# Attention stage: the log of the softmax sum goes into the row that carries the maximum; four q/k sets; one exponential for the last query tile

## The chip, the cores and the metric

One core of a Trainium2 chip runs the whole program in one launch. The metric is device microseconds of one execution. PE is TensorE, DVE is VectorE, ACT is ScalarE, POOL is GpSimd, and SP is the queue from which nearly all DMAs are issued.

## The reference, cut to what matters

Attention over 4 batches of 8 heads, 576 tokens, head size 64, float32, followed by two feed-forward parts (a dense one in `w_in`, `w_out`, then a routed one with 8 experts):

```python
cum    = np.cumsum(np.log(np.clip(f, 1e-4, 1.0)), axis=-1)
scores = q @ k.T / 8 + cum[..., :, None] - cum[..., None, :]
scores = np.where(causal, -1e9, scores)
scores = scores - np.max(scores, axis=-1, keepdims=True)
attn   = np.exp(scores)
attn   = attn / (np.sum(attn, axis=-1, keepdims=True) + 1e-9)
x      = attn @ v
x      = leaky_relu(x @ w_in) @ w_out          # 2304 tokens, 512 -> 2048 -> 512
out    = routed experts(x)                     # not touched by the change
```

## The kernel before, in words

The change lies in the first stage, attention, which also turns the first half of `w_in` (64-bit floats in memory) into 32-bit parts beside its own work. The heads go in 16 pairs, `n` = 0 to 15. The two heads of a pair lie in partitions 0 to 63 and 64 to 127. A pair has three steps:

- `prepare`: loads q and k (tile `x`), turns them on PE, and splits the result into a rounded part and a rest (`qh`, `ql`, `kh`, `kl`); ACT makes the rounded part, DVE the rest. These and two tiles of extra rows (`qr`, `kr`) make a set; there are three sets, and pair `n` uses set `(n + 2) % 3`. The rows of the cumulated logs reach `kr` by a DMA from `cumd`.
- `offsets`: scores with the queries in the partitions, in four parts (query tiles 1 and 2; 3 and 0; tile 4 in two halves of 288 keys). DVE adds the mask and takes minus the row's maximum (`kept`, `nm`; it shows as CUSTOM_DVE), ACT takes the exponential and sums it (`sm`). `rows` splits `nm` into two parts (`xh`), turns them on PE, copies them (`xr`) and writes them by two DMAs into rows of `qr`. `inverse` adds the two sums of tile 4, adds 1e-9 and takes the reciprocal (three DVE instructions on `sm`). A turn on PE, an ACT copy (`xi`), one DMA to memory (`invd`) and two that read it back over 64 partitions each fill `R`.
- `attend`: scores with the keys in the partitions, where the product with `kr`, `qr` adds the cumulated logs and minus the maximum. ACT takes the exponential (`P`), POOL clears what lies above the diagonal, PE multiplies by v (`vt`) into `av`, for 320 and then 256 queries. `finish` multiplies `av` by `R` on DVE, POOL rounds the product and subtracts (two instructions, tile `xt`), and a DMA stores both to `xd`.

All tiles of PSUM in this stage come from one ring of four (`s`). `weight_ops` loads one 128x256 piece of `w_in` (tile `w`, ring `w64`), runs three DVE instructions (`wbits`) and three on POOL (`wsq`, `wst`); there are 16 pieces here. `x_ops` loads the input of the next stage (`X` from `xd`) in two DMAs of 1 MB.

The order on each engine is written by a planner (`Plan.order`): every operation has an engine, an assumed duration, what it needs, the buffers it takes, and a rank. The planner walks through assumed time, and on each engine that is free it takes the ready operation of the lowest rank. `MOVE` holds the time it assumes from a DMA's issue to its end. `NEAR` lets PE prefer matmuls of one kind. Ranks count 12 for each pair: `prepare` of pair `n` has `12n + ZP`, `offsets` `12n + ZO`, `attend` `12n + ZA`. On the chip each engine then runs its instructions strictly in that order. Nearly all of them are issued by one helper and so stand under line 66 in the profile: they are told apart by tile.

The next stage starts with `x @ w_in` on PE (`h<-X,wh`) while `w_out` pieces are loaded (`w<-in_moe_w_out`).

Of the kernel before, what the change touches and what calls it, by code (L numbers as in the profile page):

```python
# [12 lines left out]
FT = mybir.dt.float32  # L13
# [17 lines left out]
WB = 40  # L31
W64 = 2, 6, 4
# [14 lines left out]
NEAR = 7.5  # L47
NEARB = 5
ZN = 2.5, 0, 0, 0
ZM = 0, 0, 0, 0  # L50
NK = 4
SB = 4
# [33 lines left out]
class Plan:  # L86
# [5 lines left out]
    MOVE = 650, 950  # L92
# [128 lines left out]
def tile_kernel(ctx, tc, q, k, v, f, w_in, w_out, w_gate, w1, w2, out):  # L221
# [12 lines left out]
    invd = drp.tile([B * H // 2, 12, 128], FT, name="invd")  # L234
# [25 lines left out]
    def weight_ops(op, pieces, z, st, low_on, keep=None):  # L260
# [7 lines left out]
        def chunk(c, src):  # L268
            m = {}

            def load():
                m["w"] = raw[0].tile([128, 256, 2], I32, name="w64", tag="w64", bufs=raw[1])
                sp.dma_start(m["w"].rearrange("p a b -> p (a b)"), src)
# [22 lines left out]
            o = op("sp", 450, load, (), z, ["w64"], (), 728)  # L296
# [59 lines left out]
    def w_in_ops(op, half, c, z, low_on):  # L356
        st = {}
        weight_ops(op, [(256 * u, w_in[128 * c:128 * c + 128, 2048 * half + 512 * u:2048 * half + 512 * u + 512]) for u in range(4)], z, st, low_on)
        return st
# [153 lines left out]
    with ExitStack() as c1:  # L513
# [4 lines left out]
        raw[:] = at, W64[0]  # L518
# [23 lines left out]
        def load_f():  # L542
            pre["ft"] = at.tile([hd, S], FT, name="ft", tag="xt", bufs=2)
            pre["cn"] = [at.tile([hd, S], FR, name="cn", tag="R", bufs=2) for _ in range(2)]
            sp.dma_start(pre["ft"], f.rearrange("b h s -> (b h) s"))
# [13 lines left out]
        o = op("sp", 450, load_f, (), -1000, ["R", "R", "xt"], (), 30)  # L559
        xb, fb = o.got[:2], o.got[2]  # L560
# [5 lines left out]
        for l in range(2):  # L566
            o = op("vec", 500, lambda l=l: negate(l), [o], -1000, (), [cb, xb[l]])
            cums.append(op("sp", 450, lambda l=l: sp.dma_start(cumd[l], pre["cn"][l].bitcast(FT)), [o], -1000, (), [xb[l]], 200))
# [3 lines left out]
        QH, QL, QR, KH, KL, KR = zip(*([stp.tile([128, W1], FR, name=f"{n}{i}") for n in ("qh", "ql", "qr", "kh", "kl", "kr")] for i in range(3)))  # L572
# [3 lines left out]
        for i in range(3):  # L576
            n = (i + 1) % 3
# [13 lines left out]

        heads = [(b, hp) for b in range(B) for hp in range(H // 2)]

        def prepare(n, own, z):
# [3 lines left out]
            qh, ql, kh, kl, kr = (x[(n + 2) % 3] for x in (QH, QL, KH, KL, KR))  # L598
# [59 lines left out]
            for u in range(2):  # L658
                outs[0].append(op("sp", 450, lambda u=u: sp.dma_start(kr[64 * u:64 * u + 2, :S].bitcast(FT), cumd[:, H * b + h + u]),
                                  [outs[0][0]] + cums + (pads[(n + 2) % 3] if n < 3 else []), z + 1, (), [sets[0]], 30))  # L660
            own["ready"] = outs[0] + outs[1] + (pads[(n + 2) % 3] if n < 3 else [])

        def rows(x, dst, need, z, uses, duse):

            mine = {}

            def split(l):
                if l == 0:
                    mine[0] = xh = at.tile([128, 2, 2, 5], FR, name="xh", tag="xh", bufs=2)
                    vec.tensor_copy(xh[:, :, 0], x()[:, :, :5])  # L670
                else:
                    vec.tensor_tensor(mine[0][:, :, 1], x()[:, :, :5], mine[0][:, :, 0], op=OP.subtract)

            def flip():
                mine[1] = bank()[:, 0]
                pe.transpose(mine[1][:20, :128], mine[0].rearrange("p u l t -> p (u l t)").bitcast(FT), ident)

            def copy():
                mine[2] = at.tile([20, 128], FR, name="xr", tag="xr", bufs=2)
                act.copy(mine[2], mine[1][:20, :128])  # L680
            o = op("vec", 80, lambda: split(0), need, z, ["xh"], uses)
            xh = o.got[0]
            o = op("vec", 80, lambda: split(1), [o], z, (), uses + [xh])
            o = op("pe", 107, flip, [o], z + 1, ["s"], [xh])
            st = o.got[0]
            o = op("act", 158, copy, [o], z + 2, ["xr"], [st])
            xr = o.got[0]
            return [op("sp", 450, lambda u=u: sp.dma_start(dst(u).bitcast(FT), mine[2][10 * u:10 * u + 10].bitcast(FT)), [o], z + 3, (), duse + [xr], 30) for u in range(2)]

        def offsets(n, own, z):  # L690

            qh, ql, qr, kh, kl, kr = (x[(n + 2) % 3] for x in (QH, QL, QR, KH, KL, KR))
            kq = [own["k"], own["q"]]

            def tiles():
                own["nm"] = at.tile([128, 2, 6], FT, name="nm", tag="nm", bufs=2)
                own["sm"] = at.tile([128, 2, 6], FT, name="sm", tag="sm", bufs=2)
            mins, tots = [], []

            def part(ts, z, last):  # L700
# [14 lines left out]
                def maximum(u, t, i, c0, c1, a):  # L715
# [3 lines left out]
                    if a == 0:  # L719
                        sc["kept", u] = kept[plan.kept % NK]  # L720
                        plan.kept += 1
                    vec.tensor_tensor_reduce(out=sc["kept", u][:, a:a + w], in0=sc[0][:, u, a:a + w], in1=mask[:, 448 - w:] if own_keys else mask[:, :w], scale=-1.0,
                                             scalar=nm[:, u, 5:6] if i else 3e38, op0=OP.add, op1=OP.min,
                                             accum_out=nm[:, u, t:t + 1] if own_keys else nm[:, u, 5:6])

                def total(u, t, i, c0, c1, a):
                    x = sc["kept", u][:, a:a + c1 - c0]
                    act.activation(x, x, AF.Exp, bias=own["nm"][:, u, t:t + 1], scale=-1.0, accum_out=own["sm"][:, u, t + i:t + i + 1])
# [4 lines left out]
                if first:  # L733
                    own["tiles"], own["nmb"] = o, o.got[1:]
                nb, sb = own["nmb"]
                r = []
                for u in range(2):
                    ms, hold = [], []
                    for x in ts:
# [4 lines left out]
                    r.append((ms[0], hold[0], lambda u=u: total(u, *ts[0])))  # L744
                    if ts[0][0] == 4 and ts[0][1] == 0:
                        continue
                    for x, m in zip(ts, ms):
                        tots.append(op("act", 280 + .833 * (x[3] - x[2]), lambda u=u, x=x: total(u, *x), [m], z + 2, (), hold + [nb, sb]))
                    if last:
                        tots.append(op("act", 280 + .833 * 288, last[u][2], [ms[0]], z + 2, (), [last[u][1], nb, sb]))  # L750
# [14 lines left out]
            mine = {}  # L765

            def flip():
                mine[0] = bank()[:, 0]
                pe.transpose(mine[0][:12, :128], own["sm"].rearrange("p u t -> p (u t)"), ident)

            def copy():
                mine[1] = at.tile([12, 128], FT, name="xi", tag="xi", bufs=2)
                act.copy(mine[1], mine[0][:12, :128])
            o = op("pe", 107, flip, [o], z + ZR[1] + 1, ["s"], [sb])
            o = op("act", 158, copy, [o], z + ZR[1] + 2, ["xi"], o.got)
            o = op("sp", 450, lambda: sp.dma_start(invd[n], mine[1]), [o], z + ZR[1] + 3, (), o.got, 30)
# [579 lines left out]
```

## Time and profile before

| | |
|---|---|
| median of 3 runs | 950.34 us (950.34 to 952.45) |
| the profiled execution | 950.49 us, of which 948.7 us is the span |
| busy over the span | PE 898.9 us (95%), DVE 597.6 (63%), ACT 415.1 (44%), POOL 463.9 (49%) |
| attention, in the trace | PE's first score matmul at 12.57 us, its last attention matmul ends at 220.0 us |
| mean granted PE clock | 0.979 of full speed |

The shares of the span mix stages. In the first 220 us all of PE, ACT, DVE and POOL are well filled; from there to about 460 us the feed-forward matmuls fill PE nearly alone. The profile's rows are read as: busy time of an engine in a stretch, with its number of instructions in brackets.

### The profile page before, as it was taken

How to read it: one execution, taken by the hardware profiler on the slowest of the kernel's cores; microseconds unless marked ns; L12 is line 12 of the kernel's file. 1: busy time of each engine (PE TensorE's matmuls, PEld its weight loads, DVE VectorE, ACT ScalarE, POOL GpSimd, SP SyncE). 2: the span in 40 equal slices, each digit the busy share in tenths (PEclk: the TensorE clock that was granted, in tenths of full speed). 3: DMA queues.
4: the chain of work that ended last, by engine and by line, in shares of the span. 5: the costliest groups of instructions: out<-in, count | busy, mean ns of one | idle time of the engine just before them, and what ended most of it. 6: DMA issues, size and time to landing. Idle time of an engine off the chain costs nothing.

```text
span 948.7 us, 18992 instructions
## 1 busy us (share of the span) xinstructions
PE 898.9 (95%) x6922; PEld 761.1 (80%) x6922; DVE 597.6 (63%) x1488; ACT 415.1 (44%) x1013; POOL 463.9 (49%) x570
## 2 busy tenths in 40 slices
PE   6899998998999999999999999999969999999996
PEld 5777787876777788777777777777649999999996
DVE  5787776754899459623546767566845565565631
ACT  5888887982222223322222122223314554555521
POOL 6477866556998228300545564467853121321101
PEclk9999999999999999999899999999988999999998
DMA  5566776537986456520221122112336656656511
GB/s 122 134 180 172 203 187 182 157 105 243 341 279 244 155 166 191 178 89 27 96 67 56 57 67 67 57 57 67 112 116 182 189 175 195 202 178 213 180 41 33
DMA packets 142621, 136.63 MB, mean 144 GB/s; under 512 B 69152, under 2 KB 107552, under 8 KB 142528
## 3 DMA queue, kind: packets, MB, share of 16 engines
q1 hardware_dynamic: 139456, 125.99, 43.5%
q0 software_dynamic: 3072, 9.44, 3.4%
q8 instruction: 54, 0.88, 0.4%
q14 instruction: 39, 0.32, 0.1%
HBM read 104.57 MB, written 30.65 MB: 143 GB/s over the span
## 4 chain that ended last, share of the span: by engine, by line
PE 65%; issue 11%; ACT 7%; DVE 7%; DMA 4%; POOL 4%; SPq 1%; POOLq 0%; ACTq 0%; DVEq 0%
PE acc L1017 20%; PE h L66 20%; PE h L1073 7%; PE y L1086 6%; ACT kept L66 5%; PE s L66 4%; PE T L66 3%; PE q_ct L1017 2%; DVE kept L66 2%; ACT P L66 2%; DVE wbits L66 2%; DMA w<-in_moe_w_in 2%; POOL out L1094 1%; DVE r_ge L1235 1%; SPq L66 1%
## 5 line engine op out<-in xcount | busy, mean ns | idle before, releaser
L66 PE MATMUL h<-X,wh 128*128 128x512 f32 (+1 forms) x960 | 211.2, 376 | 0.8 <-issue 0.7
L66 PEld LDWEIGHTS h<-X,wh 128*128 128x128 f32 x960 | 166.2, 190 | 38.4 <-issue 3.4
L1017 PE MATMUL acc<-wh,gh 128*128 128x512 f32 x576 | 189.1, 404 | 0.0
L453 POOL TENSOR_TENSOR gl<-g,gh 128x512 fp32r<-128x512 f32 x64 | 105.0, 1644 | 74.1 <-ACT gh L452 70.6
L1017 PEld LDWEIGHTS acc<-wh,gh 128*128 128x128 f32 x576 | 108.1, 192 | 19.4
L1073 PE MATMUL h<-XE,wh 128*128 128x288 f32 x768 | 118.5, 303 | 0.3 <-ACT XE L1064 0.3
L1017 PE MATMUL acc<-wh,gl 128*128 128x512 f32 x288 | 116.3, 404 | 0.0
L352 ACT CAST wh<-wst 128x512 fp32r<-128x512 f32 x132 | 80.5, 620 | 81.0 <-DMA wst<-in_moe_w 49.2
L66 DVE TENSOR_TENSOR wh<-wst,wh 128x512 fp32r<-128x512 f32 x132 | 91.0, 712 | 38.9 <-ACT wh L352 31.2
L1073 PEld LDWEIGHTS h<-XE,wh 128*128 128x128 f32 x768 | 106.6, 191 | 0.6 <-ACT XE L1064 0.6
L66 ACT ACTIVATE g<-h 128x512 f32<-128x512 f32 (+1 forms) x72 | 39.7, 551 | 150.6 <-PE h L66 141.0
L452 ACT CAST gh<-g 128x512 fp32r<-128x512 f32 x64 | 39.5, 621 | 140.3 <-PE acc L1017 129.2
L1086 PE MATMUL y<-eh,wh 128*128 128x288 f32 x512 | 98.3, 296 | 0.0
L66 ACT ACTIVATE kept<-kept,nm 128x192 f32<-128x192 f32 (+2 forms) x192 | 97.0, 507 | 1.9 <-DVE nm L66 1.1
L1094 POOL DMA_INDIRECT out<-yo,ids x24 | 25.9, 1078 | 129.8 <-DVE yo L1093 120.7
L66 DVE SCALAR_TENSOR_TENSOR wbits<-w,wbits 128x256 int32<-128x256 int32 x128 | 81.0, 633 | 2.9
L66 DVE TENSOR_TENSOR g<-g,h 128x512 f32<-128x512 f32 (+1 forms) x72 | 44.9, 623 | 56.5 <-ACT g L66 56.2
L1086 PEld LDWEIGHTS y<-eh,wh 128*128 128x128 f32 x512 | 79.5, 188 | 0.2 <-ACT eh L1077 0.2
L66 DVE CUSTOM_DVE_ANT_0 kept<-s,mask 128x192 f32<-128x192 f32 (+4 forms) x160 | 59.7, 422 | 21.4 <-PE s L66 18.5
L66 POOL TENSOR_TENSOR wst<-wsq,wbits 128x256 f32<-128x256 f32 x64 | 49.3, 771 | 39.6 <-DVE wbits L66 35.5
L1086 PE MATMUL y<-el,wh 128*128 128x288 f32 x256 | 67.9, 296 | 0.0
L66 ACT ACTIVATE P<-s 128x640 f32<-128x640 f32 (+1 forms) x64 | 51.7, 828 | 26.6 <-PE s L66 20.1
(200 smaller groups left out, 1682.7 us busy)
## 6 DMA issues: line engine op xcount, KB each, us to landing
wst<-in_moe_w SPq DMA_DIRECT2D x128, 256.0 KB
X<-xd SPq DMA_DIRECT2D x12, 1024.0 KB
g<-gd SPq DMA_DIRECT2D x36, 256.0 KB
w<-in_moe_w_in SPq DMA_DIRECT2D x32, 256.0 KB
w<-in_moe_w_out SPq DMA_DIRECT2D x32, 256.0 KB
gd<-g SPq DMA_DIRECT2D x16, 512.0 KB
xd<-xt SPq DMA_DIRECT2D x16, 320.0 KB
R<-invd SPq DMA_DIRECT2D x32, 144.0 KB
```

Source lines behind the costliest of these rows:

```text
L66: r = getattr(self.engine, name)(*a, **k)
L352: A.copy(r[u][0], x)
L452: A.copy(gh, g)
L453: G.tensor_tensor(gl, g, gh, op=OP.subtract)
L1017: tc.keep_in_program_order(PE.matmul(*a, **k))
L1073: PE.matmul(h[:, :CAP], w, X[:, c, x, :], start=n == 0, stop=n == 3 * NC - 1)
L1086: PE.matmul(yt[c][:, :CAP], w[:, s], a, start=j == 0 and n == 0, stop=j == NJ - 1 and n == 2)
L1094: sd = G.indirect_dma_start(out=out[:, :], out_offset=bass.IndirectOffsetOnAxis(ap=ids[:, 3 * e + t:3 * e + t + 1], axis=0), in_=y, in_off ...
L1235: V.scalar_tensor_tensor(many[:, :NT * (K + 1)].rearrange("p (i k) -> p i k", k=K + 1)[:, :, :K], key[:, :, None].to_broadcast(s), base if ...
```

## The change

What it does, in the order of the code:

- The sets become four (`NS`), pair `n` uses set `n % 4`. The first set lies in `xa`, the tile into which the next stage's input is loaded; that load now also waits for the transposed scores of pair 12 (`users`).
- The two halves of query tile 4 write one 576-wide `kept` tile, and one exponential with one sum runs over it. `kept` moves to another pool and becomes 576 wide; the ring `nm`, `sm` becomes three deep.
- `inverse`, its turn, its copy, `invd` and `R` are gone. In their place stand `guess` (DVE), `ratio` (an exponential on ACT) and `series` (six DVE instructions), which make minus the log of the sum and add it to `nm`, 128x10. `rows` turns this on PE first, then ACT rounds it and DVE subtracts, from PSUM; it thus waits for the sums too.
- `finish` no longer multiplies. For the first half DVE copies (with rounding) and subtracts, from PSUM; for the second half DVE copies to SBUF and POOL rounds and subtracts as before.
- The weights' raw tiles are four instead of two in a ring, and each of the 16 loads waits for the first score matmuls of a pair (`marks`, pairs 2 to 12).
- Ranks and planner constants change: `offsets` lies 32 ranks ahead of `attend` instead of 18; `MOVE` goes from 950 to 2200 ns; `NEAR` from 7.5 to 11.

```diff
-W64 = 2, 6, 4
+W64 = 4, 6, 4
-ZP, ZO, ZA, ZH, ZL, ZW, DW = -30.5, -13, 5, -12, 7, 66, 27
-ZS = -1, 0, 7, 1, 7, 13, 14
+ZP, ZO, ZA, ZH, ZL, ZW, DW = -38, -27, 5, -6, -14.5, 68.5, 15.5
+ZS = 7, 3.5, 7, 1, 3.5, 11.5, 15.5
-ZT = -0.5, 8.5
-ZR = 5.5, 14
+ZT = -4, 5.5
+ZR = 5
+MW = 2.5, 0.65
+FIN = ("vec", "vec"), ("vec", "gp")
-NEAR = 7.5
+NEAR = 11
+NS = 4
-    MOVE = 650, 950
+    MOVE = 650, 2200
...
-            o = op("sp", 450, load, (), z, ["w64"], (), 728)
+            o = op("sp", 450, load, hold[len(cols):len(cols) + 1], z, ["w64"], (), 728)
...
+        flat = xa.rearrange("p g c t -> p (g c t)")
+        sets = [[flat[:, W1 * i:W1 * i + W1] for i in range(6)]]
+        sets += [[stp.tile([128, W1], FR, name=f"{n}{i}") for n in ("qh", "ql", "qr", "kh", "kl", "kr")] for i in range(1, NS)]
...
-            o = op("vec", 80, lambda: split(0), need, z, ["xh"], uses)
-            xh = o.got[0]
-            o = op("vec", 80, lambda: split(1), [o], z, (), uses + [xh])
-            o = op("pe", 107, flip, [o], z + 1, ["s"], [xh])
+            o = op("pe", 107, flip, need, z + 1, ["s"], uses)
             st = o.got[0]
-            o = op("act", 158, copy, [o], z + 2, ["xr"], [st])
+            o = op("act", 145, high, [o], z + 2, ["xr"], [st])
             xr = o.got[0]
-            return [op("sp", 450, lambda u=u: sp.dma_start(dst(u).bitcast(FT), mine[2][10 * u:10 * u + 10].bitcast(FT)), [o], z + 3, (), duse + [xr], 30) for u in range(2)]
+            a = [o, op("vec", 200, low, [o], z + 2, (), [st, xr])]
+            return [op("sp", 450, lambda l=l: sp.dma_start(dst(l).bitcast(FT), mine[1][:, l].bitcast(FT)), a[l:l + 1], z + 3, (), duse + [xr], 30) for l in range(2)]
...
-                    x = sc["kept", u][:, a:a + c1 - c0]
+                    x = sc["kept", u][:, :S] if i else sc["kept", u][:, a:a + c1 - c0]
...
-                    if last:
-                        tots.append(op("act", 280 + .833 * 288, last[u][2], [ms[0]], z + 2, (), [last[u][1], nb, sb]))
...
-            own["max"] = rows(lambda: own["nm"], lambda u: qr[64 * u + 32:64 * u + 34], mins, z + ZR[0], [nb], kq)
-            o = op("vec", 530, inverse, tots, z + ZR[1], (), [sb])
...
-            a = op("sp", 625, lambda: spread(0), [o], z + ZR[1] + 4, ["R"], (), 410)
-            own["Rb"] = a.got[0]
-            own["inv"] = [a, op("sp", 625, lambda: spread(1), [o], z + ZR[1] + 4, (), a.got, 410)]
+            def guess():
+                own["ln"] = x = at.tile([128, 3, 10], FT, name="ln", tag="ln", bufs=2)
+                vec.tensor_scalar(x[:, 0], own["sm"].bitcast(I32), LN[0], LN[1], op0=OP.mult, op1=OP.add)
+            def ratio():
+                act.activation(own["ln"][:, 1], own["ln"][:, 0], AF.Exp)
+            def series():
+                x, t = own["ln"][:, 2], own["ln"][:, 1]
+                vec.scalar_tensor_tensor(t, own["sm"], 1e-9, t, op0=OP.add, op1=OP.mult)
+                vec.tensor_scalar(x, t, LN[5], LN[4], op0=OP.mult, op1=OP.add)
+                vec.tensor_tensor(x, x, t, op=OP.mult)
+                vec.scalar_tensor_tensor(x, x, LN[3], t, op0=OP.add, op1=OP.mult)
+                vec.scalar_tensor_tensor(x, x, LN[2], own["ln"][:, 0], op0=OP.add, op1=OP.add)
+                vec.tensor_tensor(x, x, own["nm"][:, :10], op=OP.add)
+            o = op("vec", 80, guess, tots, z + ZR, ["ln"], [sb])
+            lb = o.got[0]
+            p = op("act", 230, ratio, [o], z + ZR, (), [lb])
+            o = op("vec", 900, series, [p], z + ZR, (), [nb, sb, lb])
+            own["max"] = rows(lambda: own["ln"][:, 2], lambda l: qr[32 + l:97 + l:64], [o], z + ZR, [lb], kq)
...
-                o = op("vec", 69 + 1.042 * w, scale, own["inv"] + R["av", half], z, (), [Rb] + R["avb", half])
-                o = op("gp", 96 + 3.55 * w, lambda: split(0), [o], z + 1, ["xt"], [Rb])
+                o = op(first, 51 + .833 * w if first == "act" else 69 + 1.042 * w, high, R["av", half], z, ["xt"], R["avb", half])
                 xb = o.got[0]
-                o = op("gp", 148 + 2.1 * w, lambda: split(1), [o], z + 1, (), [Rb, xb])
+                if rest == "gp":
+                    o = op("gp", 96 + 3.55 * w, lambda: low(1), [o], z + 1, (), [xb])
+                    o = op("gp", 148 + 2.1 * w, lambda: low(0), [o], z + 1, (), [xb])
+                else:
+                    o = op("vec", 69 + 1.042 * w, lambda: low(0), [o], z + 1, (), [xb] + R["avb", half])
...
-        wi0 = [w_in_ops(op, 0, c, ZW + DW * c, "gp") for c in range(NC)]
-        x0 = x_ops(op, lambda: xa, WIDE1[0], ZX, stores[:H], "ex")[0]
+        wi0 = [w_in_ops(op, 0, c, ZW + DW * c, "gp", [marks[int(MW[0] + MW[1] * (4 * c + u))] for u in range(4)]) for c in range(NC)]
+        x0 = x_ops(op, lambda: xa, WIDE1[0], ZX, stores[:H] + users, "ex")[0]
```

## Rows read from the trace of the kernel before

**Rows 1.** Busy us (instructions) by stretch: PE, PEld, DVE, ACT, POOL; clock, DMA share, GB/s

```profile
12.60:41.20 28.60, 24.50 (x247) 21.49 (x247) 19.59 (x89) 25.02 (x85) 7.80 (x18) 0.94 0.49 119
41.20:106.30 65.10, 61.12 (x715) 51.40 (x713) 53.17 (x211) 55.34 (x175) 50.84 (x76) 1.00 0.67 181
106.30:160.80 54.50, 49.13 (x546) 41.88 (x542) 39.66 (x152) 43.66 (x138) 38.05 (x57) 0.94 0.73 197
160.80:205.40 44.60, 43.80 (x549) 38.33 (x547) 32.73 (x141) 41.46 (x133) 26.54 (x43) 1.00 0.45 127
205.40:220.00 14.60, 13.64 (x169) 10.99 (x167) 4.20 (x16) 8.91 (x20) 8.65 (x17) 1.00 0.54 169
```

**Rows 2.** Timeline of SP, DMA issues (start, us): one invd a pair; both X loads

```profile
41.23 0.42 SPq L66 DMA_DIRECT2D invd<-xi  x1
...
106.29 0.51 SPq L66 DMA_DIRECT2D invd<-xi  x1
...
113.36 0.57 SPq L66 DMA_DIRECT2D X<-xd  x1
...
140.49 0.57 SPq L66 DMA_DIRECT2D X<-xd  x1
...
160.76 0.50 SPq L66 DMA_DIRECT2D invd<-xi  x1
...
205.39 0.33 SPq L66 DMA_DIRECT2D invd<-xi  x1
```

**Rows 3.** Waits: us in total, times, longest; three of 41:160, the last of 160:205

```profile
PEld s L66 <- DVE R L66: 8.4, 9, 2.1
PE s L66 <- DVE R L66: 6.4, 8, 1.9
DVE wbits L66 <- DMA w<-in_moe_w_in: 5.2, 9, 1.4
...
PEld s L66 <- DVE R L66: 0.2, 1, 0.2
```

**Rows 4.** Groups by shape, 30:200 us (busy us, mean ns | idle before)

```profile
L66 ACT ACTIVATE kept<-kept,nm 128x288 f32<-128x288 f32 x55 | 28.8, 526 | 1.5 <-DVE nm L66 0.8
L66 ACT ACTIVATE kept<-kept,nm 128x448 f32<-128x448 f32 x26 | 17.0, 652 | 0.0
L66 ACT COPY xi<-s 12x128 f32<-12x128 f32 x13 | 3.1, 238 | 0.0
L66 DVE TENSOR_TENSOR R<-s,R 128x320 f32<-128x320 f32 x13 | 6.3, 482 | 0.8 <-PE s L66 0.8
L66 DVE TENSOR_TENSOR R<-s,R 128x256 f32<-128x256 f32 x13 | 5.4, 412 | 0.0
L66 DVE TENSOR_TENSOR xh<-nm,xh 128x10 fp32r<-128x10 f32 x13 | 5.7, 441 | 0.2
L66 DVE CAST xh<-nm 128x10 fp32r<-128x10 f32 x13 | 4.9, 376 | 0.2
L66 DVE TENSOR_TENSOR sm<-sm 128x2 f32<-128x2 f32 x13 | 5.0, 384 | 0.0
L66 DVE TENSOR_SCALAR sm<-sm 128x10 f32<-128x10 f32 x13 | 3.3, 250 | 0.4
L66 DVE RECIPROCAL sm<-sm 128x10 f32<-128x10 f32 x13 | 2.8, 216 | 0.4
```

**Rows 5.** Timelines of POOL and DVE: one sum blocked, one with POOL idle

```profile
109.07 2.52 POOL L66 TENSOR_TENSOR wh<-wst,wh 128x512 fp32r<-128x512 f32 x2
110.62 1.00 DVE L66 TENSOR_TENSOR sm<-sm 128x2 f32<-128x2 f32 x1
...
210.10 0.16 DVE L66 TENSOR_TENSOR sm<-sm 128x2 f32<-128x2 f32 x1 [2.39 <-ACT kept L66]
```

**Rows 6.** Chain that ended last, 205:235 us: the last pair's `R`

```profile
215.22 3.86 DMA R<-invd
```

**Rows 7.** Timeline of PE in the ramp

```profile
28.53 0.37 PE L66 MATMUL s<-ident,sm 128*12 128x128 f32 x1 [2.34 <-ACT kept L66]
```

More of the change, by code (lines that the diff above doesn't have):

```diff
@@ L258, in tile_kernel, with weight_ops @@
     tiny = float(np.array([897 << 20], np.int32).view(np.float32)[0])
-    def weight_ops(op, pieces, z, st, low_on, keep=None):
+    def weight_ops(op, pieces, z, st, low_on, keep=None, hold=()):
         cols = []
@@ L271, in load @@
             def load():
-                m["w"] = raw[0].tile([128, 256, 2], I32, name="w64", tag="w64", bufs=raw[1])
+                if isinstance(raw[0], list):
+                    raw[0].append(raw[0].pop(0))
+                    m["w"] = raw[0][-1]
+                else:
+                    m["w"] = raw[0].tile([128, 256, 2], I32, name="w64", tag="w64", bufs=raw[1])
                 sp.dma_start(m["w"].rearrange("p a b -> p (a b)"), src)
@@ L354, in split_weights, with w_in_ops @@
         return r
-    def w_in_ops(op, half, c, z, low_on):
+    def w_in_ops(op, half, c, z, low_on, hold=()):
         st = {}
-        weight_ops(op, [(256 * u, w_in[128 * c:128 * c + 128, 2048 * half + 512 * u:2048 * half + 512 * u + 512]) for u in range(4)], z, st, low_on)
+        weight_ops(op, [(256 * u, w_in[128 * c:128 * c + 128, 2048 * half + 512 * u:2048 * half + 512 * u + 512]) for u in range(4)], z, st, low_on, hold=hold)
         return st
@@ L543, in load_f @@
             pre["ft"] = at.tile([hd, S], FT, name="ft", tag="xt", bufs=2)
-            pre["cn"] = [at.tile([hd, S], FR, name="cn", tag="R", bufs=2) for _ in range(2)]
+            pre["cn"] = [kept[NK - 2 + l][:hd].bitcast(FR) for l in range(2)]
             sp.dma_start(pre["ft"], f.rearrange("b h s -> (b h) s"))
@@ L566, in tile_kernel @@
         for l in range(2):
[L567 to L572 removed]
+            o = op("vec", 500, lambda l=l: negate(l), [o], -1000, (), [cb])
+            cums.append(op("sp", 450, lambda l=l: sp.dma_start(cumd[l], pre["cn"][l].bitcast(FT)), [o], -1000, (), (), 200))
+        flat = xa.rearrange("p g c t -> p (g c t)")
+        sets = [[flat[:, W1 * i:W1 * i + W1] for i in range(6)]]
+        sets += [[stp.tile([128, W1], FR, name=f"{n}{i}") for n in ("qh", "ql", "qr", "kh", "kl", "kr")] for i in range(1, NS)]
+        QH, QL, QR, KH, KL, KR = zip(*sets)
         QO = stp.tile([128, 128], FR, name="qo")
@@ L575, in tile_kernel @@
         pads = []
-        for i in range(3):
-            n = (i + 1) % 3
+        for n in range(NS):
+            i = n
             fs = [(560, lambda i=i: gp.memset(QR[i].bitcast(FT), 0.0)), (560, lambda i=i: gp.memset(KR[i].bitcast(FT), 0.0))]
@@ L678, in copy @@
-            def copy():
-                mine[2] = at.tile([20, 128], FR, name="xr", tag="xr", bufs=2)
-                act.copy(mine[2], mine[1][:20, :128])
-            o = op("vec", 80, lambda: split(0), need, z, ["xh"], uses)
-            xh = o.got[0]
-            o = op("vec", 80, lambda: split(1), [o], z, (), uses + [xh])
-            o = op("pe", 107, flip, [o], z + 1, ["s"], [xh])
+            def flip():
+                mine[0] = bank()[:10, 0, :128]
+                pe.transpose(mine[0], x(), ident)
@@ L685, in rows, with high, low @@
+            def high():
+                mine[1] = at.tile([10, 2, 128], FR, name="xr", tag="xr", bufs=2)
+                act.copy(mine[1][:, 0], mine[0])
+            def low():
+                vec.tensor_tensor(mine[1][:, 1], mine[0], mine[1][:, 0], op=OP.subtract)
+            o = op("pe", 107, flip, need, z + 1, ["s"], uses)
             st = o.got[0]
-            o = op("act", 158, copy, [o], z + 2, ["xr"], [st])
+            o = op("act", 145, high, [o], z + 2, ["xr"], [st])
             xr = o.got[0]
-            return [op("sp", 450, lambda u=u: sp.dma_start(dst(u).bitcast(FT), mine[2][10 * u:10 * u + 10].bitcast(FT)), [o], z + 3, (), duse + [xr], 30) for u in range(2)]
+            a = [o, op("vec", 200, low, [o], z + 2, (), [st, xr])]
@@ L733, in part @@
                 if first:
+                    marks.append(o)
                     own["tiles"], own["nmb"] = o, o.got[1:]
@@ L738, in part @@
                     ms, hold = [], []
+                    if last:
+                        hold = [last[u][1]]
                     for x in ts:
@@ L765, in offsets @@
[L765 to L776, printed above, removed]
@@ L866, in finish, with high @@
-                Rb = own["Rb"]
-                o = op("vec", 69 + 1.042 * w, scale, own["inv"] + R["av", half], z, (), [Rb] + R["avb", half])
-                o = op("gp", 96 + 3.55 * w, lambda: split(0), [o], z + 1, ["xt"], [Rb])
-                xb = o.got[0]
-                o = op("gp", 148 + 2.1 * w, lambda: split(1), [o], z + 1, (), [Rb, xb])
+                first, rest = FIN[half]
+                def high():
+                    own["x", half] = x = at.tile([128, 2, 320], FR, name="xt", tag="xt", bufs=2)
+                    to = x[:, 1, :w].bitcast(FT) if rest == "gp" else x[:, 0, :w]
+                    if first == "act":
+                        act.copy(to, own["av", half][:, :w])
+                    else:
+                        vec.tensor_copy(to, own["av", half][:, :w])
```

101 lines of the change are left out of this document (45 added, 56 removed).

## The prediction

> **What bounds the kernel now.** I first looked for the stretch that the change can reach. PE takes its last attention matmul at 220.0 us, and what follows is left as it is, so the question is how long attention lasts. The busy times by stretch show that no engine is alone there [rows 1], so I cut the stretches at the `invd` issue that each pair makes once [rows 2]. From 41.23 to 106.29 us five pairs pass, 13.0 us each; to 160.76 us four, 13.6 each; to 205.39 us four more, 11.15 each. In the last of these PE is busy 43.8 of 44.6 us: 98%, so 11.15 us is what PE needs for a pair, and there PE is the bound [rows 1]. In the two earlier ones, where the pieces of `w_in` are turned, no engine is at its limit for long: per pair DVE is busy 10.6 and 9.9 us, against 8.2 in the clean stretch (32.73/4), ACT 11.1 and 10.9 against 10.4 [rows 1]. The time above PE's need is 5 x 1.85 + 4 x 2.45 = 19 us. That is what could be won there; the ramp before 41 us and the end after 205 us are looked at below.
>
> The waits say how it is lost [rows 3]. From 41 to 160 us PE waits for `R` on DVE, the instruction that empties a PSUM tile, for 6.4 us and its weight loads for 8.4; from 160 to 205 us the weight loads wait 0.2. DVE runs in order, and in the same time it stood 5.2 us at the head of its queue until a piece of `w_in` had landed, with `R` and the maxima behind it. Both 1 MB loads of `X` also lie in this stretch, at 113.36 and 140.49 us [rows 2], and the second stretch is the one with a PE clock of 0.94 of full speed and a DMA share of 0.73, against 1.00 and 0.67 in the first [rows 1].
>
> **The change part by part.** All figures are us a pair unless said otherwise.
>
> ACT: four exponentials of 288 columns go (4 x 0.526), two of 576 come. From 288 to 448 columns the mean grows by 0.126, so 0.79 ns a column, and 576 columns come to 0.652 + 128 x 0.00079 = 0.753, as an estimate from these two rows [rows 4]. That saves 2.10 - 1.51 = 0.6. The copy `xi` (0.24) goes, and `ratio`, an exponential of ten columns, comes at about the same. ACT falls from 10.4 to 9.8 in a clean pair. ACT was not what ended the pair there, so by itself this is worth nothing; it is room.
>
> DVE, out: `xh` 0.376 + 0.441, `sm` 0.384 + 0.250 + 0.216, `R` 0.482 + 0.412, together 2.56 [rows 4]. In: `guess` as the one-input `sm` row, 0.25; `series`, five instructions with two tile inputs at 0.384 to 0.441 and one at 0.25, 2.17 to 2.46; the subtraction in `rows`, between 0.216 and 0.441; in `finish` a copy and a subtraction of 320 columns and a copy of 256 from PSUM, for which `R` at the same widths stands, 2 x 0.482 + 0.412 = 1.38. That is 4.0 to 4.5, net +1.45 to +1.95 at the durations of a busy stretch. With POOL idle the small sum took 0.16 [rows 5]; eight new small ones at that price and five old ones gone give +0.97. Since POOL loses two of its four `xt` instructions a pair, I take +1.3; ends 0.97 and 1.95.
>
> At 110.62 us the sum on `sm`, two inputs in SBUF, took 1.00 us while POOL ran two subtractions from 109.07 to 111.59, and 0.16 us with POOL idle [rows 5]. The Trainium skill (SBUF — State Buffer, "Who interferes with whom") says that a DVE instruction with two SBUF inputs and a GpSimd instruction that reads SBUF exclude each other for a whole instruction; the trace agrees, with 0.84 us between these rows. It speaks against this change: two such small instructions a pair become five.
>
> The weights' share of DVE is 10.6 - 8.2 = 2.45 over nine pairs; the marks spread the same 16 pieces over pairs 2 to 12, eleven, which makes 2.0. So DVE in a pair with weights comes to 8.2 + 1.3 + 2.0 = 11.5. That is over PE's 11.15: in these pairs DVE is late next. How full an in-order DVE can run is the unknown. It was 82% full in the first stretch (53.17 of 65.1) with two raw tiles and waits at its head; PE reached 98% in the clean one. Four raw tiles and an assumed DMA time that is 1.25 us longer move `wbits` behind the landing of its piece, and the `R` read, for which `R` stood, is gone. I take 93%, nearer to the clean row because the named waits go: 11.5/0.93 = 12.4. Nine pairs then take 111.6 us instead of 119.6: **-8.0 us**. Ends: 11.0 (PE alone) and 14.0 (11.5 at 82%).
>
> The `X` loads now wait for pair 12, about three pairs before the end. By then the rows and sets of pairs 13 to 15 are mostly made, and PE has their transposed scores and values to do; I cost them at nothing. If that cover is gone, the price is bounded by what the second stretch lost against the first, 4 x 0.6 = 2.4 us, or, if all of that stretch's excess was theirs, 9.8.
>
> The clean pairs: PE loses one turn of ten columns. The one row for it shows 0.37 at a low clock [rows 7]; below it nothing. I take 0.15, four pairs: **-0.6 us**. SP loses three of its issues a pair; no row shows PE waiting for SP itself, so nothing.
>
> The end: the last pair's `R` waited for a DMA of 3.86 us [rows 6] that ran beside PE's last work, and the last store and the first pieces of `w_out` on SP came behind it. This read is gone and the copy needs only `av`. Ends 0 and -3.9; I take **-1.5 us**.
>
> The ramp: the row that releases the first `attend` now stands behind all sums, `guess`, `ratio` and `series`. Eight steps of 0.25 to 0.44 make 2 to 3.5 us. But PE already stood 2.34 us at 28.53 us behind the turn of the sums [rows 7], and with a fourth set it has one more pair's scores (`offsets`) to run meanwhile. Ends -2.3 and +4; I take **+0.5 us**. Later the added wait is covered by the distance of 32 ranks, 2.7 pairs; what queues behind the waiting turn is all of PE, so the planner's order must hold.
>
> Sum: -8.0 - 0.6 - 1.5 + 0.5 = -9.6 us, against the profiled execution of 950.49 us (span 948.7, with 1.8 around it), which stands 0.15 us above the median: 940.9, so 941 us.
>
> **The rivals.**
> - PE alone is the bound: the 19 us came from the `X` loads and the waits for DMA only, and DVE's extra work fits beside them. Nine pairs at 11.2 give -18.8 us, with the smaller terms 930 us. For it: without weights the kernel does run at 98% of PE. Against it: DVE at 11.5 is over this pace.
> - The wait only changes its name: PE waits for the copy out of `av` as it waited for `R`, since both stand in the same DVE queue. Then only the `X` loads' 2.4 us go, about 948 us. For it: the 14.8 us in rows 3 are waits for DVE's turn. Against it: pieces land earlier relative to their use.
> - DVE makes it slower: its share stays 82%, as in the first stretch, and 11.5/0.82 = 14.0 us for each of nine pairs, +6.4 us, with the ramp at +2 some 958 us. It decides from where DVE runs less than 11.5/13.3 = 86% full in the pairs with weights. For it: five small instructions in a chain that POOL can block (at 0.84 us each for all five, DVE would need 4 us more). Against it: the same in-order queue without DMA waits, and POOL has less to do.
>
> **How the numbers follow.** About 0.3%, 3 us, is what a measurement of this kernel can tell from no change. Chances: the forecast 0.55 (its own range 932 to 947), PE alone 0.17, changed name 0.12, slower 0.16. The range 926 to 956 takes in most of the bounds of the pace and of the ramp; below it only 11.0 us in every pair, above it the full slow case. Faster 0.72, same 0.12, slower 0.16.
>
> **What would show it.** In the changed profile: pairs with weights at 12.0 to 12.8 us, DVE over 90% busy there; clean pairs at 11.0; ACT below 10 a clean pair; two exponentials of 576 columns near 0.75 us; no PE wait of several us at the `X` loads; first `attend` within 3 us of before; attention's last matmul near 210 us. The forecast is wrong if pairs with weights keep 13 us or more, or if the ramp costs more than 4 us; after 220 us nothing should change but the start of the `w_out` pieces.

## The result, and the profile after

The changed kernel takes 942.12 us (median of 4 runs, 939.5 to 943.29) against 951.39 us for the kernel before in the same comparison: ratio 0.9896, 95% interval 0.9866 to 0.9927. The forecast was 941.

The profiled execution took 943.13 us, with a span of 941.1. PE's last attention matmul ends at 213.4 us instead of 220.0, and the span is 7.6 us shorter: 6.6 us in attention, 1.0 behind it. The stretches below are cut where PE turns the row of a pair (`s<-ident,ln`, once a pair): from 42.20 us nine pairs with weights pass to 156.39, then three to 190.78 that hold no more than one piece ("clean" below). They answer to [rows 1]: busy us (instructions) of PE, PEld, DVE, ACT, POOL; then clock, DMA share, GB/s.

```profile
12.60:42.20 29.60, 24.96 (x258) 22.08 (x254) 25.47 (x123) 26.07 (x88) 11.77 (x28) 0.94 0.51 122
42.20:156.40 114.20, 104.31 (x1245) 90.78 (x1243) 105.95 (x398) 93.80 (x279) 71.20 (x111) 0.99 0.55 147
156.40:190.80 34.40, 33.40 (x417) 30.04 (x415) 29.25 (x117) 30.96 (x93) 14.82 (x27) 1.00 0.42 111
190.80:213.40 22.60, 22.36 (x274) 18.54 (x274) 8.99 (x32) 13.63 (x27) 10.28 (x22) 1.00 0.64 195
```

A pair with weights now takes 12.7 us instead of 13.3, and in those pairs DVE is busy 105.95 of 114.2 us, 92.8%: it is late next. PE is idle 9.9 us of them (114.20 - 104.31), no less than the 9.35 before (119.6 - 110.25); what fell is its busy time. A clean pair takes 11.5 us, PE being 97% busy. The waits from 41 to 160 us answer to [rows 3] (us in total, times, longest). A line of PEld and one of PE can tell of the same stop, so the two do not add up:

```profile
PEld s L71 <- DVE nm L71: 11.1, 14, 2.2
PE s L71 <- DVE nm L71: 8.2, 13, 2.0
...
DVE wbits L71 <- DMA w<-in_moe_w_in: 0.4, 1, 0.4
```

DVE no longer stands before a piece of `w_in` (5.2 us before, 0.4 now), and `R` is gone. But PE still waits for DVE to empty a PSUM tile, 8.2 us where it waited 6.4 for `R`; the instruction that does it is now the maximum (`nm`). The groups by shape from 30 to 200 us answer to [rows 4] (busy us, mean ns | idle before):

```profile
L71 ACT ACTIVATE kept<-kept,nm 128x576 f32<-128x576 f32 x28 | 21.3, 763 | 0.0
L71 DVE SCALAR_TENSOR_TENSOR ln<-ln 128x10 f32<-128x10 f32 x30 | 11.7, 391 | 1.0
L71 DVE CAST xt<-s 128x320 fp32r<-128x320 f32 x14 | 6.7, 480 | 0.5 <-DMA xd<-xt 0.5
L71 DVE TENSOR_TENSOR xt<-s,xt 128x320 fp32r<-128x320 f32 x13 | 6.3, 484 | 0.1
L71 DVE SCALAR_TENSOR_TENSOR ln<-sm,ln 128x10 f32<-128x10 f32 x15 | 5.6, 371 | 1.1 <-ACT ln L71 1.1
L71 DVE COPY xt<-s 128x256 f32<-128x256 f32 x13 | 5.4, 415 | 0.0
L71 DVE TENSOR_TENSOR ln<-ln,nm 128x10 f32<-128x10 f32 x15 | 5.3, 353 | 0.5
L71 DVE TENSOR_SCALAR ln<-ln 128x10 f32<-128x10 f32 x15 | 4.4, 292 | 0.5
L71 DVE TENSOR_TENSOR xr<-s,xr 10x128 fp32r<-10x128 f32 x15 | 4.1, 276 | 2.4 <-ACT xr L71 2.4
L71 DVE TENSOR_SCALAR ln<-sm 128x10 f32<-128x10 int32 x14 | 4.0, 288 | 0.7 <-ACT kept L71 0.7
L71 DVE TENSOR_TENSOR ln<-ln 128x10 f32<-128x10 f32 x15 | 3.2, 212 | 0.5
```

What the change put on DVE is `guess` 0.288, `series` 2 x 0.391 + 0.371 + 0.353 + 0.292 + 0.212 = 2.01, `xr` 0.276 and `finish` 0.480 + 0.484 + 0.415 = 1.38: 3.95 us a pair, of which 2.56 replace what went: +1.39 at the means of this long stretch. Both `X` loads are now issued at 188.43 us. The ten microseconds from there (same columns as above) show the DMA engines 92% busy and a PE that hardly notices (98% busy):

```profile
188.43 1.28 SPq L71 DMA_DIRECT2D X<-xd  x2
```

```profile
188.00:198.00 10.00, 9.76 (x126) 8.57 (x124) 7.08 (x33) 9.20 (x27) 3.16 (x7) 1.00 0.92 281
```

### The profile page after: what moved, and what is told of

The parts are those of the page before. It is cut to its first block, busy times and chain, and to the rows that moved or that the text cites. A ratio compares the mean times of both kernels' runs of the same rounds, so it can differ in the third digit from the quotient of the medians.

```text
span 941.1 us, 19011 instructions
## 1 busy us (share of the span) xinstructions
PE 893.4 (95%) x6906; PEld 759.8 (81%) x6906; DVE 609.9 (65%) x1552; ACT 407.2 (43%) x949; POOL 438.4 (47%) x548
## 4 chain that ended last, share of the span: by engine, by line
PE 69%; DVE 11%; issue 11%; POOL 4%; ACT 3%; DMA 1%; POOLq 0%; SPq 0%; ACTq 0%; DVEq 0%
PE acc L1031 21%; PE h L71 21%; PE h L1087 7%; PE s L71 7%; PE y L1100 6%; PE T L71 3%; DVE kept L71 3%; DVE ln L71 3%; PE q_ct L1031 2%; DVE wbits L71 2%; ACT kept L71 2%; POOL out L1108 1%; DVE r_ge L1249 1%; DVE xt L71 1%; PE T L1077 1%
## 5 line engine op out<-in xcount | busy, mean ns | idle before, releaser
L71 ACT ACTIVATE kept<-kept,nm 128x192 f32<-128x192 f32 (+4 forms) x160 | 87.8, 551 | 17.1 <-DVE nm L71 16.9
L71 DVE TENSOR_TENSOR g<-g,h 128x512 f32<-128x512 f32 (+1 forms) x72 | 44.6, 621 | 51.9 <-ACT g L71 51.9
L71 DVE SCALAR_TENSOR_TENSOR wbits<-w,wbits 128x256 int32<-128x256 int32 x128 | 75.3, 589 | 2.8
L1031 PEld LDWEIGHTS acc<-wh,gl 128*128 128x128 f32 x288 | 55.4, 192 | 9.8
L71 POOL TENSOR_SCALAR wsq<-wsq 128x256 f32<-128x256 f32 x64 | 59.9, 935 | 5.6
```

Of the source, the lines that this page charges most:

```text
L71: r = getattr(self.engine, name)(*a, **k)
L1031: tc.keep_in_program_order(PE.matmul(*a, **k))
```

## The experiments

All ratios are to the kernel before, measured beside it on the same chip, with 95% intervals. Two changed versions are compared by these ratios, since most were not measured side by side. What is read from a profile is one execution of each. The first experiments ask where the gain came from, the later ones (from `series` twice on) what holds the changed kernel.

**Late `X` loads alone.**

```diff
+                if pair == 12:
+                    users.append(o)
...
-        x0 = x_ops(op, lambda: xa, WIDE1[0], ZX, stores[:H], "ex")[0]
+        x0 = x_ops(op, lambda: xa, WIDE1[0], ZX, stores[:H] + users, "ex")[0]
```

> The kernel before with one edit: the two X loads of 1 MB also wait for the transposed scores of pair 12. Theory A (the gain of the change has several small sources: X loads out of the stretch with weights, no waits of DVE for pieces at its head, room on ACT, and DVE's extra work takes a part back): 2.4 to 5 us faster than before, since the second stretch of four pairs loses at least 0.6 us a pair more than the first. Rival B (the X loads alone were the loss): 7 to 10 us faster, all that the change gave. Rival C (weights ring and assumed DMA time gave it): within 1 us of before.

Measured 947.55 us, ratio 0.996 (0.9941 to 0.998): 3.8 us faster. Theory A holds, B and C fall. Nine pairs with weights take 115.9 us here instead of 119.6, though DVE's waits for pieces do not fall (6.6 us against 5.2). In their new place the loads are not free in this kernel: PE stands 2.0 us for a row (`qr`) whose DMA was issued at 186.75 us, right behind them.

```profile
41.40:157.30 115.90, 107.50 (x1257) 91.25 (x1255) 92.32 (x362) 98.38 (x312) 89.59 (x133) 0.99 0.65 176
```

```profile
184.60 1.30 SPq L66 DMA_DIRECT2D X<-xd  x2
186.75 1.52 SPq L66 DMA_DIRECT2D qr<-xr  x2
```

```profile
194.22 0.65 PE L66 MATMUL s<-qr,kr 64*128 64x320 f32 x2 [2.01 <-DMA qr<-xr]
```

**Four raw tiles and 2200 ns.**

```diff
-W64 = 2, 6, 4
+W64 = 4, 6, 4
-    MOVE = 650, 950
+    MOVE = 650, 2200
```

> The kernel before with two constants: four raw weight tiles instead of two, and an assumed DMA end of 2200 ns instead of 950. Theory A: about 3 us faster (DVE's 5.2 us of waits for pieces go, and some of PE's waits for R behind them). Rival B: within 1 us. Rival C: 6 to 8 us faster.

Measured 942.84 us, ratio 0.9912 (0.9887 to 0.9937): 8.4 us faster, just over theory C's 6 to 8; A had it too small, B falls. Waits of its 41 to 160 us:

```profile
PEld s L66 <- DVE R L66: 5.4, 9, 1.5
PE s L66 <- DVE R L66: 3.4, 5, 1.3
...
DVE wbits L66 <- DMA w<-in_moe_w_in: 0.9, 2, 0.5
```

DVE's waits for pieces fall from 5.2 to 0.9 us, and the waits for `R` from 6.4 to 3.4 us on PE and from 8.4 to 5.4 on its weight loads, though `R`, its DMAs and three sets are all still there.

**Each of these constants alone** (the edit is one of the two pairs of lines above).

> The kernel before with one constant: the assumed end of a DMA goes from 950 to 2200 ns, two raw tiles stay. Ring and constant together gave 8.4 us (0.9912). Theory A2 (the order was written for DMAs that land 1.25 us too early, so engines stood at the head of their queues): most of it, 4 to 7 us faster than before. Theory A3 (two raw tiles kept the pieces late, the assumed time matters little): under 2 us.

> The kernel before with four raw weight tiles instead of two, the assumed DMA end stays 950 ns. Theory A2: under 3 us faster. Theory A3: 6 to 8 us faster.

Measured 945.7 us, 0.9943 (0.9921 to 0.9965), with the assumed DMA time alone, and 946.95 us, 0.9947 (0.9925 to 0.9968), with the ring alone. The two are worth about the same, 0.0057 and 0.0053 of the time, and together gave 0.0088, most of their sum. Theory A2 met the assumed time (4 to 7 us) and missed the ring (under 3); A3 missed both. DVE's waits for pieces fall to 0.8 and 1.4 us.

But the two act in different places. With the assumed time alone, nine pairs with weights take 121.0 us, no less than before (119.6), and attention ends at 219.7 us instead of 220.0: nothing is won there. `MOVE` belongs to the planner, which also writes the order of the next stage. In the kernel before, PE runs 36 matmuls of that stage and then stops twice for the turns of `w_out` pieces that POOL makes (`wst`); with 2200 ns it runs 48 and stops there for 0.27 us. From attention's end to the end of the stage's last matmuls (`acc<-sel`) it takes 243.5 us instead of 247.7. The other profiles bear this out: 246.6 to 249.3 us in every kernel here with 950 ns, 243.3 to 246.3 in every one with 2200. The ring alone ends attention 4.3 us earlier, at 215.7. The first three rows are the kernel before, the next two and the stretch the one with 2200 ns:

```profile
220.00 8.69 PE L66 MATMUL h<-X,wh 128*128 128x512 f32 x36
230.46 0.44 PE L66 MATMUL T<-ident,wst 128*128 128x128 f32 x2 [1.78 <-POOL wst L66]
232.95 0.60 PE L66 MATMUL T<-ident,wst 128*128 128x128 f32 x2 [2.05 <-POOL wst L66]
```

```profile
220.25 11.51 PE L66 MATMUL h<-X,wh 128*128 128x512 f32 x48 [0.53 <-DVE R L66]
232.25 0.44 PE L66 MATMUL T<-ident,wst 128*128 128x128 f32 x2 [0.27 <-POOL wst L66]
```

```profile
39.70:160.70 121.00, 110.35 (x1274) 94.53 (x1276) 94.38 (x363) 99.11 (x314) 87.74 (x130) 0.96 0.67 181
```

**Both edits and the late loads together, no log, no fourth set.**

> The kernel before with both edits (late X loads; four raw tiles and 2200 ns). Theory A: 6 to 9 us faster, the two gains add, pairs with weights near 12.4 us. Rival B: as the late X loads alone. Rival C: as the ring alone. If it is as fast as the changed kernel, then the log, the fourth set and the single exponential brought nothing by themselves.

Measured 939.98 us, ratio 0.9881 (0.9856 to 0.9905): 11.3 us faster, over theory A's 6 to 9 and near the sum of the two gains. The intervals do not separate it from the changed kernel (0.9896): three small edits give as much, and the log, the fourth set, the single exponential and the new ranks together add nothing to it that these runs can tell. In attention alone the changed kernel is ahead, though: it ends there at 213.4 us, this one at 215.0, and the rest of the time makes up for it. Nine pairs with weights of this kernel (same columns as above):

```profile
40.40:151.30 110.90, 106.90 (x1276) 91.95 (x1278) 91.62 (x364) 99.37 (x316) 90.76 (x134) 0.98 0.65 174
```

They take 12.3 us each, less than the 12.7 of the changed kernel, with DVE 83% busy and PE idle 4.0 us.

**The changed kernel with the old assumed DMA time.**

```diff
-    MOVE = 650, 2200
+    MOVE = 650, 950
```

> The changed kernel with the assumed DMA end back at 950 ns, four raw tiles stay. Theory A2: 4 to 8 us slower than the changed kernel, near the kernel before. Theory A3: within 2 us of the changed kernel.

Measured 953.36 us, ratio 1.0028 (1.0011 to 1.0046): some 12 us over the changed kernel by the ratios. The whole gain goes, and more than theory A2 expected (4 to 8). Its pairs with weights, then its clean ones:

```profile
44.30:162.60 118.30, 107.02 (x1244) 92.58 (x1242) 108.29 (x401) 93.08 (x276) 70.42 (x111) 0.97 0.54 144
162.60:201.00 38.40, 35.21 (x415) 30.20 (x415) 28.19 (x115) 31.59 (x94) 15.45 (x29) 1.00 0.38 101
```

13.1 and 12.8 us a pair. DVE's waits for pieces are only 2.6 us here, so most of the loss is not such a wait: the whole order differs, in the clean pairs too. Attention ends at 223.7 us instead of 213.4, so here most of the loss lies in attention. How it divides among the transfers was not taken apart.

**One exponential for the last tile, in the kernel before.**

```diff
...
-                    x = sc["kept", u][:, a:a + c1 - c0]
+                    x = sc["kept", u][:, :S] if i else sc["kept", u][:, a:a + c1 - c0]
...
```

> The kernel before with one exponential of 576 columns for the last query tile instead of two of 288 (and kept and raw tiles in the places where the changed kernel has them; the addition of the two sums becomes a copy). Theory A: ACT is 0.6 us a pair shorter but ends no pair, within 2 us of before. Rival D (ACT was a bound beside PE): 0.6 us for each of 16 pairs, 8 to 10 us faster.

Measured 953.66 us, ratio 1.0028 (1.0009 to 1.0047). Less work on ACT is no gain here; theory D falls. The small loss need not come from the exponential, since the edit also moves tiles and changes the order; which of these it is was not tried.

**`series` twice, in the changed kernel.**

```diff
+                vec.scalar_tensor_tensor(r, own["sm"], 1e-9, t, op0=OP.add, op1=OP.mult)
+                vec.tensor_scalar(y, r, LN[5], LN[4], op0=OP.mult, op1=OP.add)
...
+                vec.tensor_tensor(y, y, own["nm"][:, :10], op=OP.add)
```

> The changed kernel with the six instructions of series run a second time into a scratch tile (same shapes and inputs). The changed kernel has DVE 92.8% busy over the nine pairs with weights (105.95 of 114.2 us). Theory A (DVE is the bound in the pairs with weights): six instructions at 0.2 to 0.4 us add 1.3 to 2.2 us of DVE a pair and the run gets 10 to 20 us slower than the changed kernel. Rival E (PE or the order is the bound, a busy DVE is only its symptom): under 3 us slower.

Measured 972.38 us, ratio 1.0235 (1.0211 to 1.026): about 30 us over the changed kernel, past theory A's 10 to 20. Its pairs with weights, then its clean ones:

```profile
45.65:180.79 135.14, 117.26 (x1282) 99.31 (x1278) 122.18 (x457) 96.90 (x280) 70.92 (x113) 0.90 0.46 125
180.79:221.90 41.11, 35.84 (x416) 30.99 (x415) 35.81 (x141) 31.52 (x93) 14.79 (x26) 0.96 0.37 102
```

DVE has 13.6 us of work in a pair with weights instead of 11.8, and the pair takes 15.0 instead of 12.7. Each microsecond added to DVE costs more than one. Not all of that is DVE's own time: PE's clock is 0.90 of full speed here against 0.99, and with 3% more instructions PE is 13 us longer busy. Theory A holds in direction; E falls.

**`series` on POOL.**

```diff
-                vec.scalar_tensor_tensor(t, own["sm"], 1e-9, t, op0=OP.add, op1=OP.mult)
-                vec.tensor_scalar(x, t, LN[5], LN[4], op0=OP.mult, op1=OP.add)
+                gp.tensor_tensor(t, own["sm"], t, op=OP.mult)
+                gp.tensor_scalar(x, t, LN[5], LN[4], op0=OP.mult, op1=OP.add)
...
-            o = op("vec", 900, series, [p], z + ZR, (), [nb, sb, lb])
+            o = op("gp", 2400, series, [p], z + ZR, (), [nb, sb, lb])
```

> The changed kernel with series on POOL (eight small instructions there, the 1e-9 left out) instead of six on DVE. Theory A: DVE loses 1.9 us a pair, pairs with weights go from 12.7 to about 11.6 us, 6 to 10 us faster than the changed kernel. Rival E: within 2 us, or slower, since POOL's small instructions are slow and the chain to the row gets longer.

Measured 938.45 us, ratio 0.9881 (0.9857 to 0.9904): 1.4 us below the changed kernel by the ratios, which the intervals don't separate, and less than theory A's 6 to 10. From 81.4 us six pairs with weights, and the new POOL instructions from 30 to 200 us (busy us, mean ns | idle before):

```profile
81.40:151.60 70.20, 66.53 (x830) 59.13 (x828) 57.86 (x226) 62.68 (x185) 59.45 (x123) 1.00 0.60 160
```

```profile
L71 POOL TENSOR_SCALAR ln<-ln 128x10 f32<-128x10 f32 x44 | 10.6, 242 | 3.8
L71 POOL TENSOR_TENSOR ln<-ln 128x10 f32<-128x10 f32 x44 | 9.3, 211 | 3.7
```

Those six pairs run at 11.7 us, as theory A has it, with DVE 82% and PE 95% busy. The four before them took 50.1 us where the changed kernel took 47.5: what was won late was lost early.

**The same with ranks that suit it.**

```diff
-ZP, ZO, ZA, ZH, ZL, ZW, DW = -38, -27, 5, -6, -14.5, 68.5, 15.5
-ZS = 7, 3.5, 7, 1, 3.5, 11.5, 15.5
+ZP, ZO, ZA, ZH, ZL, ZW, DW = -42.5, -27, 5, -9, -14.5, 68.5, 16
+ZS = 7, 4, 7, 1, 0.5, 11.5, 15.5
-ZT = -4, 5.5
+ZT = -4.5, 4
-MW = 2.5, 0.65
+MW = 2.5, 0.6
```

> The changed kernel with series on POOL (as before, the 1e-9 left out) and ranks that suit it: prepare 4.5 ranks earlier, the marks of the pieces at 0.6 instead of 0.65 of a pair, five smaller shifts. With the ranks unchanged, pairs 5 to 11 already ran at 11.7 us instead of 12.7, but one stop of PE near 65 to 70 us cost some 3 us, where DVE stood before pieces that were issued three at a time. Theory A (DVE's extra work is what held the changed kernel): 2 to 5 us faster than with the ranks unchanged, 935 us, faster than both kernels. Rival E: no faster than 938 us, the order's quality decides.

Measured 937.16 us, ratio 0.9845 (0.9822 to 0.9868): the fastest version here, by its ratio 4.8 us below the changed kernel (the intervals just touch), and clear of the kernel before. Against the ranks unchanged it is 3.4 us by the ratios, which theory A allows (2 to 5), but the intervals overlap, and 937.16 lies only just below rival E's 938: the two are not told apart. Nine pairs with weights, then three clean ones:

```profile
41.10:151.10 110.00, 101.64 (x1244) 89.69 (x1242) 91.83 (x346) 95.00 (x282) 92.09 (x189) 1.00 0.57 153
151.10:185.30 34.20, 33.54 (x417) 29.84 (x415) 22.39 (x96) 30.57 (x92) 17.73 (x51) 1.00 0.39 102
```

12.2 us instead of 12.7 with weights, for 1.6 us of DVE taken away (91.83/9 = 10.2 against 11.77): what comes off DVE is not won in full. The clean pairs stay at 11.4, so there DVE was not what held the changed kernel.

**The first copy of `av` on ACT.**

```diff
-FIN = ("vec", "vec"), ("vec", "gp")
+FIN = ("act", "vec"), ("act", "gp")
```

> The changed kernel with the first copy of av of both halves on ACT instead of DVE. DVE loses 0.48 + 0.42 us a pair, ACT gains about 0.75 (from 10.3 to 11.0 in pairs with weights). Theory A: 3 to 6 us faster than the changed kernel if ACT does not become the bound. Rival E: no change. Rival D (ACT is as close to the bound as DVE): 0 to 5 us slower.

Measured 943.97 us, ratio 0.9931 (0.9907 to 0.9954): not faster, nearer to theory D. Its pairs with weights, then its clean ones, from an execution of 949.13 us, well above its own median:

```profile
44.26:156.68 112.42, 103.32 (x1245) 90.81 (x1243) 100.40 (x380) 99.70 (x297) 69.01 (x110) 1.00 0.57 149
156.68:195.92 39.24, 36.58 (x416) 31.64 (x415) 29.76 (x111) 33.59 (x100) 14.75 (x26) 0.91 0.36 96
```

With weights 12.5 us, ACT at 89%; the clean pairs took 13.1 there, at a clock of 0.91. Whether that is ACT or that one execution stays open.

**Three sets instead of four.**

```diff
-NS = 4
+NS = 3
```

> The changed kernel with three q/k sets in a place of their own instead of four (the X loads still wait for pair 12). Theory A: the row now needs all sums, the log and a DMA before attend; with three sets the distance of 32 ranks can not be kept, PE waits for rows or for q and k: 8 to 25 us slower than the changed kernel, slower than before. Rival F (the fourth set is not needed): within 3 us of the changed kernel.

Measured 995.67 us, ratio 1.0482 (1.0457 to 1.0507), far past theory A's upper end. Nine pairs take 16.6 us each. No engine is full: PE is 80% busy, DVE 68%, ACT 63%, and the granted clock is 0.87. That the pairs wait for one another there is argued from this, not traced. The ranks are still those made for four sets, so this is not the price of three sets with ranks of their own:

```profile
37.90:187.40 149.50, 119.96 (x1258) 99.03 (x1255) 102.35 (x397) 94.67 (x281) 70.68 (x113) 0.87 0.45 120
```

## Why the prediction was right, and where it was not

**The pairs with weights.** The step was: DVE comes to 11.5 us a pair, runs 93% full, the pair takes 12.4, -8.0 us. Measured: 11.77 us, 92.8%, 12.7 us, 114.2 instead of 119.6, -5.4 us. The fullness is met; the mis-sized term is DVE's work. Without `wbits` (rows below: nine pairs before, then after) DVE has 86.3/9 = 9.6 us a pair against 72.1/9 = 8.0 before, +1.6 where +1.3 was taken (ends 0.97 and 1.95). The weights' share is 2.2, where 2.0 was taken. (In these pairs it was 2.3 before; the 2.45 was read from the first five alone.) That more work on DVE is paid in full is shown by `series` run twice; that less work there is won in part, by `series` on POOL.

```profile
L66 DVE SCALAR_TENSOR_TENSOR wbits<-w,wbits 128x256 int32<-128x256 int32 x30 | 15.3, 510 | 0.1
L66 DVE TENSOR_SCALAR wbits<-w 128x256 int32<-128x256 int32 x14 | 5.4, 390 | 5.7 <-DMA w<-in_moe_w_in 5.2 <-POOL wst L66 0.5
```

```profile
L71 DVE SCALAR_TENSOR_TENSOR wbits<-w,wbits 128x256 int32<-128x256 int32 x28 | 14.8, 529 | 0.4
L71 DVE TENSOR_SCALAR wbits<-w 128x256 int32<-128x256 int32 x14 | 4.9, 353 | 0.5 <-DMA w<-in_moe_w_in 0.4
```

**The total.** The sum was -9.6 us. By the medians it is -9.3, between the two profiled executions, for which it was worked out, -7.4. That 941 was met so closely is in part luck.

**What gave the gain.** The waits at DVE's head were named, and they went, 5.2 to 0.4 us. But I priced them as one story with the lost `R` read and the room on ACT. The runs separate them: in the kernel before, the assumed DMA time gives about 5 us, the ring 5, the late loads 4, and all three together 11.3 (0.9881). The assumed time alone gives its part in the next stage, where the sum had not looked. In total time the algebra of the change is then worth nothing measurable, and the single exponential alone was not a gain.

PE's account of nine pairs with the same matmuls of `P` and `x` shows why. PE is busy 110.3 us before, 106.9 with the three edits, 104.3 in the changed kernel; it is idle 9.4, 4.0 and 9.9 us. So the change does take work from PE, and PE gives the time back in stops, most of them for DVE's `nm`: DVE's addition. Part of PE's lower busy time is its clock. Before, PE twice ran for about 3.4 us at the lower level, 0.50 of full speed (1.2 instead of 2.4 GHz), each time after a stretch with long stops, as here:

```profile
115.00:120.00 5.00, 2.70 (x24) 1.71 (x23) 3.57 (x11) 1.78 (x11) 3.89 (x6) 1.00 1.02 304
120.00:124.00 4.00, 3.79 (x27) 3.73 (x29) 1.37 (x8) 2.54 (x6) 1.45 (x3) 0.57 0.58 158
```

In the changed kernel this happens once in the nine pairs, near 144 us, after PE had stopped for 2.0 us. Two matmuls of 320 columns start 0.15 us after the two before them at 119.26 us and 0.27 us at 122.72, so such a stretch costs some 1.5 us, as an estimate from these rows. What makes up the rest was not taken apart.

**The `X` loads** cost nothing at 188 us, as forecast. Their price in the old place was bounded by 2.4 and 9.8; the run that moved them alone gives 3.8 in all, 3.7 in the nine pairs, with 2.0 us of PE lost behind them in the new place. The cover that makes them free belongs to the changed kernel.

**The clean pairs** were to win 0.15 us each, from 11.15 to 11.0; they take 11.46. The fault is in the 11.15 that I took for PE's need of a pair. In both stretches PE turns q and k of three pairs (27 turns), but the old stretch has four pairs and the new one three:

```profile
L66 PE MATMUL s<-ident,x 128*128 128x128 f32 x27 | 4.0, 275 | 0.0
L71 PE MATMUL s<-ident,x 128*128 128x128 f32 x27 | 3.5, 275 | 0.0
```

With the fourth pair's turns at the price of the others (4.0/3 = 1.3 us, an estimate), the old pace is (44.6 + 1.3)/4 = 11.5: no loss, and no gain that shows. ACT's 10.4 has the same fault. In the clean pairs ACT has 10.3 us, not 9.8; in those with weights it falls from 11.0 to 10.4, the 0.6 that was forecast. The 19 us above PE's need were thus read some 3 us too large.

**The ramp** was +0.5. PE has 258 instructions in 29.6 us against 247 in 28.6 [rows 1], and is idle 4.6 us against 4.1, which fits. But the first product with `vt` starts at 43.78 us instead of 36.98, 6.8 us later where at most 3 was forecast. PE runs more of `offsets` first, as the forecast had it: 48 matmuls of `qo` with the rows of k, four pairs' worth, against 32. That the ramp rests on the fourth set is not shown: with three sets this product starts at 38.21 us, and that kernel loses its 5.9% in the pairs behind it.

**The end** was -1.5, for the lost `R` read. From attention's end to the end of the last `acc<-sel` the changed kernel takes 245.6 us instead of 247.7, of which 1.1 us is lost again later. But the assumed DMA time alone, with the `R` read in place, brings this stretch to 243.5. So the size is near, and what is shown to shorten it is the constant; the read was not tried by itself.

**The rivals.** PE alone as the bound did not come: DVE runs at 92.8%. The wait that changes its name came as a mechanism: PE now waits 8.2 us for `nm` where it waited 6.4 for `R` [rows 3], in shorter pieces (13 times 0.6 us on the mean, against 8 times 0.8), and is as long idle as before. Its time, 948 us, did not come. The slower case asked for DVE under 86% full; it was above. (With the smaller terms it adds up to 957 us, not 958.) The rule of the Trainium skill (SBUF — State Buffer, "Who interferes with whom") bears on `series`: with POOL's `wh` subtractions beside them, two of its instructions took 2.54 us together. The trace agrees there. It does not for the instruction before them: with two inputs in SBUF it took 0.17 us, though POOL was rounding `xt`, also from SBUF (spans on POOL are rough):

```profile
111.04 0.98 POOL L71 TENSOR_SCALAR xt<-xt 128x256 fp32r<-128x256 f32 x1 [2.79 <-DVE xt L71]
111.81 0.17 DVE L71 TENSOR_TENSOR ln<-ln 128x10 f32<-128x10 f32 x1
111.99 2.54 POOL L71 TENSOR_TENSOR wh<-wst,wh 128x512 fp32r<-128x512 f32 x2
112.01 2.54 DVE L71 SCALAR_TENSOR_TENSOR ln<-ln 128x10 f32<-128x10 f32 x2
```

The means of 0.21 to 0.39 us, over 0.17, show that some of them are held up, not all.

## What to carry to other kernels

When a change bundles an algebraic step with constants of the order, try the constants alone on the old kernel first: here four raw tiles, a longer assumed DMA time in the planner and a later bulk load gave 1.2%, as much as the whole change. Look in every stage where such a constant acts: the assumed time alone won nothing in the stage under study. When three engines are all near full, price a change by the one it loads, take its busy time per iteration over the fullness that the trace shows to be possible, and do not count work taken from an engine that ends nothing. Before two stretches are compared pair by pair, count that both hold the same work. A planner's assumed latency is itself a tuning knob: 1.25 us of it was worth 5 us in one kernel and 12 in the other (1.0028 against 0.9896). How much of such a gain is the luck of another order, no run here shows; the run with one exponential, 2.7 us slower with less work, warns that it can be a few microseconds.

## What was not expected of the hardware

Instructions over 128x10 cost POOL no more than DVE in this kernel: 0.21 to 0.24 us on the mean on POOL, 0.21 to 0.39 us on DVE in the same stretch of the changed kernel. That is DVE beside a busy POOL; undisturbed it takes 0.17, and POOL needed eight instructions for DVE's six. For such tiny tiles the choice of engine could here go by which one had room.
